# A third landing tile for the feeds of a middle transform stage, and a row norm queued behind the rounding of the row before

## The chip, the core and the metric

One core of a Trainium2 chip runs the whole program. The metric is the device time of one launch in microseconds (us). The engines have separate queues, each run in order: TensorE (PE; its weight loads are shown as PEld), VectorE (DVE), ScalarE (ACT), GpSimd (POOL) and SyncE (SP). A transfer is issued from the queue of SP, ACT or POOL, and all transfers share the core's 16 DMA engines.

## The reference

Four layers of two kinds are interleaved on x of 2048 rows and 576 columns, each with a layer norm ahead of it and a residual around it. Layer A is a two-dimensional Fourier transform by matrices, of which the real part is kept. Layer B is a short convolution of k, a product with v, a long convolution in the frequency domain, and a gate q, which is the normed x here; k, v and the kernels are inputs.

```
def A(x):   a = x @ hid_re.T;  b = x @ hid_im.T
            return seq_re @ a - seq_im @ b
def B(q):   kv = short_conv(k, shift_k) * v
            y  = irfft(rfft(kv, 2S) * rfft(ssm_k, 2S))[:S] + kv * ssm_D
            return q * y
x = x + A(norm(x));  x = x + B(norm(x));  x = x + A(norm(x));  x = x + B(norm(x))
```

The long convolution's result y depends on no x, so it is computed once and used in both B layers. All inputs are float32, and matrix products are made to nearly that precision.

## The kernel before

*Precision.* Every matrix operand is split into a rounded high part (ACT, a copy that rounds) and a low part (DVE, the difference); a product is then three matmuls: high x high, high x low, low x high. `split` (line 94, its operations at lines 95 and 96) does it for the c matrices of the sequence transform and for results; `to_x` (lines 188 to 194) does it for a row of x: rounding at line 190 on ACT, the difference at lines 192 and 193 on DVE.

*The main stream.* `layer` (line 306) runs the first A layer: 4 blocks of 512 outputs by 2 (real, imaginary) by 16 steps. A step loads one c tile (`load_c`, line 209, from the SP queue), splits it, and multiplies it with one row tile of x: 14 matmuls of 512 columns. In the first 16 steps the row tiles themselves are made: `get_x0` (line 680) loads a tile, takes its statistics, ends its norm (`next(ln, 0)`, line 689, which issues the scaling on ACT at line 186 for the first eight tiles, at line 665 for the others) and splits it with `to_x`. It works up to three tiles ahead of the step (XLEAD). The last A layer, from about 760 us on, uses seven products in place of eight.

*The side stream.* Between the matmuls of the main stream a generator, `branch` (line 353), computes the long convolution as a transform in three stages, a piece at each `yield`. A pacing loop (lines 761 to 780) advances it by the step of the main stream.
- The first stage (names f1r, f1f; f1_split, f1_products) takes the rows of ssm_k and of the short convolution, which runs on DVE at lines 398 and 403, multiplies them by constants f1c and stores the results to a DRAM tensor t, half by half (lines 454 and 455, issued on ACT).
- The middle stage (tile `mid`) has 64 pieces of work. Each reads one 128x576 piece of t, a "feed": `load_feed` issues its load on SP behind the latest c load (`load_after`, line 161) into a landing tile, `split_feed` makes its two halves (ACT at line 512 or 514, DVE at line 518), `mid_kernel` multiplies one column half and copies it about on ACT, `mid_signal` multiplies the other and combines both on DVE (lines 531 to 534), and `mid_round` and `mid_inverse` transform back and store to vd.
- The last stage ("i2") reads vd in 32 feeds by the same ring of landing tiles; `i2_products` multiplies a feed with constants i2c that `load_fc` brings from the POOL queue (`load_fr`, line 165) into a ring "fc" of two tiles. The first of these feeds comes behind 38 of the middle stage's, and from there every third is one.

*Rings and places.* Tiles lie at hand-chosen places in a few large buffers; `lay` (line 128) appends such places to a named ring, and a ring gives its tiles out in turn. In the middle stage "land" has two tiles, in `flts`, and "fc" has two, at the end of the buffer `mid` (lines 491 to 495). A feed's load waits for the split of the feed that had its tile.

*What sets the order.* The engines' orders are made by a scheduler from the order of the code and the dependences; `behind(...)` (line 99) and `load_after` add the rule that an instruction stands behind a given one. Lists hold such instructions: `rounded` the roundings of line 190, `stored` the last copies of line 454, `halved`, `evac` and `added` others.

Of the kernel before, what the change touches and what calls it, by code (L numbers as in the profile page):

```python
# [10 lines left out]
F32 = mybir.dt.float32  # L11
# [4 lines left out]
P = 128  # L16
S = 2048
D = 576
# [28 lines left out]
I2_FIRST = 37  # L47
# [21 lines left out]
def fnet_h3_kernel(ctx: ExitStack, tc: tile.TileContext, x, c_mat, w_re, w_im, k_pad, v, shift_k,  # L69
# [28 lines left out]
    @contextmanager  # L98
    def behind(*instructions):
        with ExitStack() as stack:  # L100
            for i in instructions:
                stack.enter_context(tc.issue_after(i))
            yield
# [11 lines left out]
    def region_b(dt, name):  # L115
        return sb.tile([P, 6 * WIDE], dt, tag="rb", name=name)
# [9 lines left out]
    ring = {}  # L126

    def lay(t, at, *sizes):

        for name, words, n in sizes:  # L130
            ring.setdefault(name, Ring()).tiles.extend(t[:, at + i * words:at + (i + 1) * words] for i in range(n))
            at += n * words
        assert at <= t.shape[1], (at, t.shape, sizes)
        return at

    def fresh(*names):
        for name in names:
            ring[name] = Ring()
# [20 lines left out]
    anchor, made, rounded, pows, biased, halved, added, evac, parted, stored = [], [], [], [], [], [], [], [], [], []  # L159

    def load_after(dst, src):
        with tc.issue_after(anchor[-1]):
            return nc.sync.dma_start(dst, src).ins

    def load_fr(dst, src):
        with tc.issue_after(pows[-1]):
            nc.gpsimd.dma_start(dst, src)
# [20 lines left out]
    def to_x(y, j):  # L188
        t = xs[:, j, :]
        rounded.append(nc.scalar.activation(t[:, :D], y, AF.Copy).ins)  # L190
        h = t.bitcast(F32)
        nc.vector.tensor_tensor(t[:, D:D + REM], y[:, NC * P:], h[:, NC * P:D], OP.subtract)
        made.append(nc.vector.tensor_tensor(t[:, D + REM:], y[:, :NC * P], h[:, :NC * P], OP.subtract).ins)
        return t
# [155 lines left out]
    def quads(v):  # L350
        return v.rearrange("p (a q) -> p a q", a=4)

    def branch():
# [3 lines left out]
        at = lay(flts, SC_AT + CRAW * NT, ("so", D, 4), ("land", D, 3))  # L357
# [126 lines left out]
        m1 = region_b(FR, "mid")  # L484
        kk_at = SC_AT + CRAW * NT + 4 * D
        at = lay(m1, 0, ("df", 2 * D, 3), ("mc", 4 * P, 1))
# [4 lines left out]
        ring["craw"].tiles.extend(held)  # L491
        spare = at
        at = lay(m1, at, ("yf", D, 2))
        lay(m1, at, ("fc", 4 * P, 2))
        at = lay(flts, SC_AT + CRAW * NT, ("res", D, 2))
        lay(flts, at, ("land", D, 2), ("kk", D, 2), ("vo", HD, 3), ("p2", HD, 1))
        mc = quads(ring["mc"]())
# [22 lines left out]
        def mid_kernel(df):  # L520
            pk, kk = mid_half(df, HD), two(ring["kk"]())
            act(kk[:, 0, :], pk[:, :HD], AF.Copy)
            act(kk[lo, 1, :], kk[hi, 0, :], AF.Copy)
            act(kk[hi, 1, :], kk[hi, 0, :], AF.Copy, scale=-1.0)
            act(kk[hi, 0, :], kk[lo, 0, :], AF.Copy)
            return kk

        def mid_signal(df, kk):
            px = mid_half(df, 0)
            p1, p2 = kk[:, 0, :], ring["p2"]()  # L530
            nc.vector.tensor_tensor(p1, px[:, :HD], p1, OP.mult)
            nc.vector.tensor_tensor(p2[lo], px[hi, :HD], kk[hi, 1, :], OP.mult)
            nc.vector.tensor_tensor(p2[hi], px[lo, :HD], kk[lo, 1, :], OP.mult)
            nc.vector.tensor_tensor(p1, p1, p2, OP.add)
            return p1

        def mid_round(p1):
            yf = two(ring["yf"]())
            act_split(yf[:, 0, :], yf[:, 1, :], p1)
            return yf  # L540

        def mid_inverse(hf, qg, yf):
            pv = bank()
            mm(pv[:, :HD], mc[:, 2, :], yf[:, 0, :], True, False)
            mm(pv[:, :HD], mc[:, 2, :], yf[:, 1, :], False, False)
            mm(pv[:, :HD], mc[:, 3, :], yf[:, 0, :], False, True)
            vo = ring["vo"]()
            act(vo, pv[:, :HD], AF.Copy)
            nc.scalar.dma_start(v_d[hf][4 * qg:4 * qg + 4].rearrange("q j c d -> (q j c) d"), vo)

        def i2_products(hf, j, fc, vf):
            yo = ring["vo"]()
            ps = bank()
            for c in range(2):
                cs = slice(c * HD, (c + 1) * HD)
                mm(ps[:, :HD], fc[:, c, :], vf[0][:, cs], c == 0, False)
                mm(ps[:, :HD], fc[:, c, :], vf[1][:, cs], False, False)
                mm(ps[:, :HD], fc[:, 2 + c, :], vf[0][:, cs], False, c == 1)
            act(yo, ps[:, :HD], AF.Copy)
            nc.scalar.dma_start(yb_d[j][:, hf * HD:(hf + 1) * HD], yo)  # L560
# [13 lines left out]
        def load_feed(i):  # L574
            if i < len(feeds):
                kind, hf, q = feeds[i]
                landed[i] = ring["land"]()
                load_after(landed[i], v_d[hf][:, q].rearrange("p c d -> p (c d)") if kind else
                           t_d[hf][4 * q:4 * q + 4].rearrange("x h j s d -> (x h j) (s d)"))

        def load_fc(k):
            if k < len(rows):
                fcs[k] = quads(ring["fc"]())
                load_fr(fcs[k], i2c[rows[k]])

        def split_feed(i):
            if i < len(feeds):
                halves[i] = parts("df")
                act_split(*halves[i], landed.pop(i))

        load_feed(0)
        load_feed(1)
        yield 0
        for i in range(2):
            split_feed(i)
            load_feed(i + 2)
            load_fc(i)
        used, ahead, product = 0, 2, None
        for i, (kind, hf, q) in enumerate(feeds):
            df = halves.pop(i)  # L600
            if kind:
                i2_products(hf, q, fcs.pop(used), df)
                load_fc(used + ahead)
                used += 1
            else:
                if len(yfs) == MID_LAG:
                    mid_inverse(*yfs.pop(0))
                    yield 0.4
                kk = mid_kernel(df)
                if product is not None:  # L610
                    yfs.append((*product[:2], mid_round(product[2])))
                yield 1.6
                product = hf, q, mid_signal(df, kk)
            split_feed(i + 2)
            load_feed(i + ahead + 2)
            if i == last_mid:
                yield 0.4
                mid_inverse(*yfs.pop(0))
                yfs.append((*product[:2], mid_round(product[2])))
                while yfs:  # L620
                    yield 0.4
                    mid_inverse(*yfs.pop(0))
                for name, t, at, words in (("fc", m1, spare, 4 * P), ("land", flts, kk_at, D)):
                    old = ring[name]
                    held = [old.tiles[(old.n + m) % 2] for m in range(2)]
                    fresh(name)
                    lay(t, at, (name, words, 2))
                    ring[name].tiles.extend(held)
                for m in range(2):
                    load_fc(used + ahead + m)  # L630
                    load_feed(i + ahead + 3 + m)
                ahead = 4
            yield I2_COST if kind else 1.1

    def sums(src, junk):
# [33 lines left out]
    def load_x(j):  # L669
        if j < J:  # L670
            XL[j] = ring["x"]()
            nc.sync.dma_start(XL[j], x[:, j, :])

    def stats0(j):
        if j < J and j not in LN:
            src = XL.pop(j)
            LN[j] = src, normed_x(src, src, ring["junk"]()) if j >= ASTAT else normed(src, src)
            next(LN[j][1])

    def get_x0(j):  # L680
        if X[j] is None:
            if j > 0:
                load_x(j + 2)
            stats0(j)
            if j > 0:
                with behind(*stored):
                    stats0(j + 1)
            src, ln = LN[j]
            next(ln, 0)
            X[j] = to_x(src, j)  # L690

    def done0(j, xa):
# [41 lines left out]
    pending = []  # L734
    lay(flts, SC_AT, ("craw", NT, CRAW))
    br = branch()
    wl = load_w()
    load_x(0)
    next(br)
    get_x0(0)  # L740
    with tc.issue_after(biased[0]):
        next(br)
# [6 lines left out]
    used = 4  # L749
# [3 lines left out]
    with behind(first_lo):  # L753
        get_x0(1)
# [243 lines left out]
    for n, whole in layer(get_x1, lambda j: xb_d[j], done1, pending, 1):  # L998
# [12 lines left out]
        if n == STATIC:  # L1011
            t7.append(region_a(FR, "t7"))
            at = lay(flts, SC_AT + CRAW * NT, ("csum", WIDE, 3), ("rems", 2 * REM, 2))
# [132 lines left out]
```

## Time and profile before

| what | value |
|---|---|
| runs of the kernel, three | 1206.66, 1211.91, 1214.1 us; median 1211.91 us |
| the profiled execution, its own time | 1212.36 us |
| its span, first to last instruction | 1210.6 us |
| mean granted TensorE clock in it | 0.995 of full |
| busy share: PE, PEld, DVE, ACT, POOL | 97%, 84%, 72%, 57%, 6% |
| moved by DMA | 271.38 MB, mean 224 GB/s |
| the chain that ended last, by engine | PE 73%, DVE 9%, ACT 7%, DMA 6%, issue 4% |

A time in a row of the timeline is that from the span's start. Such a row reads: start, duration, engine (with q: issued by its sequencer, a transfer), line, operation, output<-inputs, shape, count, and in brackets the engine's idle time just before and what ended it. The releaser is inferred, and where several were waited for it is the last one by the clock. A row "L96" or "L163" is the line of a helper, so the tile names tell what it is: "flts<-t" from SP is a feed's load, "flts<-in_c_mat" a load of a c tile, "mid<-in_i2c" from POOL a load of i2c, and "mid<-flts" on ACT (128x576) the split of a feed. Matmuls overlap in PE's pipeline: with work at hand those of 512 columns follow each other every 0.226 us, though one lasts 0.39.

### The profile page before, as it was taken

What the parts mean: (1) busy time and instruction counts of PE and PEld (TensorE: products, weight loads), DVE (VectorE), ACT (ScalarE), POOL (GpSimd) and SP (SyncE); (2) the same over time, 40 slices, a digit from 0 to 9 for tenths busy, and PEclk for the clock granted to TensorE, in tenths of its full rate; (3) what the DMA queues carried; (4) which work ended last, traced back from release to release, by engine and by line L of the source; (5) the groups of instructions that cost most, each with busy time, mean ns of one, the idle gap of its engine ahead of it and who ended that gap; (6) DMA issues with size and microseconds to landing.
All of it is one profiled execution on the core that took longest, in us unless ns stands there. A gap on an engine that the chain in (4) does not pass through costs nothing.

```text
span 1210.6 us, 18119 instructions
## 1 busy us (share of the span) xinstructions
PE 1175.5 (97%) x6192; PEld 1011.4 (84%) x6192; DVE 870.4 (72%) x1531; ACT 684.6 (57%) x1366; POOL 71.2 (6%) x116
## 2 busy tenths in 40 slices
PE   7999999989999999999999999999999999999997
PEld 5877788869888887888888898788888888889997
DVE  7799999668787777777346766775776777774764
ACT  7955666667787687767455667534444445450210
POOL 2100000000000000000111111000000000001111
PEclk9999999999999999999999999999999999999999
DMA  8878797885477477766986777873683587795621
GB/s 289 284 213 244 243 324 238 305 259 153 149 232 267 136 200 251 239 194 217 336 263 224 236 240 238 268 254 92 178 289 99 178 288 266 239 331 154 224 91 40
DMA packets 148702, 271.38 MB, mean 224 GB/s; under 512 B 16129, under 2 KB 45057, under 8 KB 148610
## 3 DMA queue, kind: packets, MB, share of 16 engines
q1 hardware_dynamic: 105266, 215.02, 55.3%
q10 hardware_dynamic: 36432, 42.63, 10.2%
q0 software_dynamic: 6912, 12.59, 4.0%
q8 instruction: 48, 0.79, 0.3%
q14 instruction: 44, 0.36, 0.1%
HBM read 198.81 MB, written 71.37 MB: 223 GB/s over the span
## 4 chain that ended last, share of the span: by engine, by line
PE 73%; DVE 9%; ACT 7%; DMA 6%; issue 4%; SPq 0%; POOL 0%; ACTq 0%; POOLq 0%; DVEq 0%
PE s L78 41%; PE bk L78 29%; PE rm L78 4%; ACT flts L512 3%; DVE f1f L398 2%; DMA flts<-in_c_mat 1%; DMA t<-flts 1%; DVE f1f L403 1%; DMA flts<-t 1%; DVE mats L96 1%; ACT mats L95 1%; ACT mid L512 1%; DVE f1r L442 1%; DVE mid L518 1%; DVE u L96 1%
## 5 line engine op out<-in xcount | busy, mean ns | idle before, releaser
L78 PE MATMUL s<-mats 128*128 128x512 f32 x2088 | 537.7, 394 | 6.5 <-DVE u L96 2.7
L78 PEld LDWEIGHTS s<-mats 128*128 128x128 f32 x2088 | 385.2, 189 | 82.4 <-DVE u L96 3.6
L95 ACT ACTIVATE mats<-flts 128x512 fp32r<-128x512 f32 x206 | 128.3, 628 | 84.9 <-PE bk L78 30.4
L96 DVE TENSOR_TENSOR mats<-flts,mats 128x512 fp32r<-128x512 f32 x206 | 140.6, 689 | 48.3 <-ACT mats L95 47.2
L78 PE MATMUL bk<-mid 128*128 128x288 f32 x768 | 134.8, 304 | 11.0 <-ACT flts L512 4.9
L78 PEld LDWEIGHTS bk<-mid 128*128 128x128 f32 x768 | 113.4, 188 | 34.0 <-ACT flts L512 15.8
L518 DVE TENSOR_TENSOR mid<-flts,mid 128x576 fp32r<-128x576 f32 (+1 forms) x160 | 102.1, 638 | 41.8 <-ACT mid L512 31.7
L78 PE MATMUL bk<-w,u 128*128 128x288 f32 x864 | 120.6, 295 | 1.1 <-ACT flts L512 0.9
L78 PEld LDWEIGHTS bk<-w,u 128*128 128x128 f32 x864 | 117.3, 188 | 4.4 <-ACT flts L512 2.3
L512 ACT ACTIVATE flts<-bk 128x288 f32<-128x288 f32 x160 | 61.2, 403 | 73.3 <-PE bk L78 59.1
L512 ACT ACTIVATE mid<-flts 128x576 fp32r<-128x576 f32 (+1 forms) x159 | 87.1, 582 | 17.0 <-DMA flts<-t 10.8
L78 PE MATMUL rm<-mats 128*128 128x512 f32 x304 | 95.8, 392 | 0.5 <-DVE flts L269 0.5
L512 ACT ACTIVATE flts<-flts 64x288 f32<-64x288 f32 x192 | 85.0, 443 | 6.2 <-ACT flts L512 0.2
L454 ACT ACTIVATE flts<-bk 128x288 f32<-128x288 f32 x128 | 46.7, 408 | 38.1 <-PE bk L78 33.2
L78 PE MATMUL bk<-mats 128*128 128x288 f32 (+1 forms) x376 | 67.8, 317 | 0.0
L78 PEld LDWEIGHTS rm<-mats 128*128 128x128 f32 x304 | 57.2, 189 | 12.6 <-PE s L78 0.9
L78 PE MATMUL s<-t,mats 128*128 128x512 f32 x264 | 64.9, 389 | 0.0
L283 DVE TENSOR_TENSOR flts<-flts,bk 128x288 f32<-128x288 f32 x48 | 21.8, 453 | 55.9 <-PE bk L78 55.1
L78 PE MATMUL bk<-mats,t 128*128 128x288 f32 (+1 forms) x368 | 59.3, 303 | 0.0
L179 POOL TENSOR_TENSOR flts<-flts 128x1 f32<-128x1 f32 x35 | 28.5, 813 | 514.7 <-DVE flts L178 514.7
L78 PEld LDWEIGHTS bk<-mats 128*128 128x128 f32 x376 | 55.6, 188 | 3.4
L78 PEld LDWEIGHTS s<-t,mats 128*128 128x128 f32 x264 | 49.5, 188 | 10.4 <-DVE t L96 0.2
(145 smaller groups left out, 1516.0 us busy)
## 6 DMA issues: line engine op xcount, KB each, us to landing
flts<-in_c_mat SPq DMA_DIRECT2D x148, 256.0 KB, 3.8
ph<-in_c_mat SPq DMA_DIRECT2D x54, 512.0 KB, 4.0
t<-flts ACTq DMA_DIRECT2D x64, 288.0 KB, 4.5
flts<-t SPq DMA_DIRECT2D x64, 288.0 KB, 3.1
flts<-in_c_mat SPq DMA_DIRECT2D x30, 512.0 KB, 5.3
vd<-flts ACTq DMA_DIRECT2D x64, 144.0 KB, 2.5
flts<-vd SPq DMA_DIRECT2D x32, 288.0 KB, 5.0
mid<-in_i2c POOLq DMA_DIRECT2D x32, 256.0 KB, 5.8
```

Source lines behind the costliest of these rows:

```text
L78: nc.tensor.matmul(ps, lhsT, rhs, start=first, stop=last, skip_group_check=more)
L95: a = nc.scalar.activation(h, src, AF.Copy).ins
L96: return a, nc.vector.tensor_tensor(l, src, h.bitcast(F32), OP.subtract).ins
L179: pows.append(nc.gpsimd.tensor_tensor(rs, ve, mhalf, OP.pow).ins)
L283: added[:] = [nc.vector.tensor_tensor(r[:, cs], r[:, cs], ps[:, :HD], OP.add).ins]
L398: nc.vector.tensor_tensor(out_t[:, n], k, wt[3 - t][:, n], OP.mult)
L403: nc.vector.tensor_tensor(rp, rp, out_t, OP.add)
L442: parted[:] = h + [nc.vector.tensor_tensor(t[to], r[at], t[at].bitcast(F32), OP.subtract).ins for t, at, to in sides]
L454: stored[:] = [nc.scalar.activation(so[:, h, :], ps[:, :HD], AF.Copy).ins]
L512: last_act.append(nc.scalar.activation(*args, **kw).ins)
L518: nc.vector.tensor_tensor(l, src, h.bitcast(F32), OP.subtract)
```

## The change

Two edits. The first lets the middle stage start with three landing tiles. The third tile takes the place at the end of `mid` that the two fc tiles had, which are not laid out until later; the two loads of i2c at the start of the stage go. Three feeds are loaded at the start, and then each feed's load is issued one feed earlier than before: behind the split of feed i+2, feed i+5 in place of i+4. From feed 29 on, as soon as the tile next in turn is the third one (that is at feed 30), the ring goes back to its other two tiles, the fc tiles are laid out, the two i2c loads are issued, one load is left out, and all goes on as before. The second edit puts the end of a row's norm (`next(ln, 0)`) behind the rounding of the row before it.

```
@@ branch @@
-        lay(m1, at, ("fc", 4 * P, 2))
+        fc_at = at
...
-        load_feed(0)
-        load_feed(1)
+        third = m1[:, fc_at:fc_at + D].bitcast(F32)
+        ring["land"].tiles.append(third)
+        for i in range(3):
+            load_feed(i)
         yield 0
         for i in range(2):
             split_feed(i)
-            load_feed(i + 2)
-            load_fc(i)
-        used, ahead, product = 0, 2, None
+            load_feed(i + 3)
+        used, ahead, feed_ahead, product = 0, 2, 3, None
...
             split_feed(i + 2)
-            load_feed(i + ahead + 2)
+            if i >= I2_FIRST - 8 and feed_ahead == 3:
+                tiles = [ring["land"]() for _ in range(3)]
+                if tiles[0] is third:
+                    ring["land"], feed_ahead = Ring(tiles[1:]), 2
+                    lay(m1, fc_at, ("fc", 4 * P, 2))
+                    load_fc(0)
+                    load_fc(1)
+            if feed_ahead == 2:
+                feed_ahead = 2.5
+            else:
+                load_feed(i + int(feed_ahead) + 2)
...
-                ahead = 4
+                ahead = feed_ahead = 4
@@ get_x0 @@
-            next(ln, 0)
+            with behind(*rounded[-1:]):
+                next(ln, 0)
             X[j] = to_x(src, j)
```

## The prediction

> **What bounds the kernel now.** I read the page first, for the busy shares; then busy time by stretch, for the places where TensorE stands still; then the timeline and the waits of those places; then the instruction orders of the two programs, which show what the edits move.
>
> ```profile
> PE 1175.5 (97%) x6192; PEld 1011.4 (84%) x6192; DVE 870.4 (72%) x1531; ACT 684.6 (57%) x1366; POOL 71.2 (6%) x116
> ...
> L512 ACT ACTIVATE mid<-flts 128x576 fp32r<-128x576 f32 (+1 forms) x159 | 87.1, 582 | 17.0 <-DMA flts<-t 10.8
> ```
>
> TensorE (PE) is busy for 1175.5 of 1210.6 us. No edit touches a matmul, so all that can be won is idle time of PE, 35.1 us, and time in which its clock is low. The second row is the work that the landing tiles feed: ACT's splits in the middle stage idled 10.8 us for transfers. Busy time by stretch (stretch, length, then busy us of PE, PEld, DVE, ACT and POOL, the granted clock, the DMA share, GB/s) tells where that is:
>
> ```profile
> 0.00:50.00 50.00, 42.03 (x175) 33.74 (x176) 33.96 (x105) 41.78 (x81) 10.81 (x21) 1.00 0.87 307
> 50.00:70.00 20.00, 17.63 (x81) 14.24 (x79) 17.68 (x30) 14.88 (x30) 2.13 (x3) 1.00 0.67 197
> 70.00:140.00 70.00, 67.03 (x306) 53.92 (x307) 68.86 (x82) 40.68 (x82) 3.18 (x6) 0.98 0.76 227
> 140.00:248.00 108.00, 107.44 (x533) 91.05 (x532) 90.00 (x109) 73.48 (x153) 4.24 (x8) 1.00 0.89 288
> 248.00:275.00 27.00, 22.94 (x101) 17.77 (x100) 17.59 (x32) 17.63 (x34) 0.00 (x0) 0.94 0.81 247
> 275.00:403.00 128.00, 125.59 (x745) 110.09 (x745) 100.65 (x203) 97.85 (x222) 0.00 (x0) 1.00 0.62 196
> 403.00:600.00 197.00, 190.67 (x1103) 166.32 (x1102) 139.18 (x268) 140.84 (x308) 12.19 (x23) 1.00 0.73 225
> 600.00:1210.60 610.60, 602.14 (x3159) 524.25 (x3157) 402.46 (x709) 257.44 (x460) 38.64 (x55) 1.00 0.65 211
> ```
>
> Length less PE busy: 8.0 us idle up to 50, 2.4 up to 70, 3.0 up to 140, 0.6 up to 248, 4.1 in the 27 us in which the middle stage opens, 2.4 in its first part, 6.3 in its second, 8.5 in the second half of the program. The two orders differ only up to about 130 us and from 254 to 403 us; behind that every engine runs the same list. So the change has some 20 us of idle within its reach, much of it the start (first loads), which it does not touch.
>
> **The change part by part.** *The norm behind the rounding (line 689).* Rows of the first layer are normed (line 186, later 665) and rounded (line 190) on ACT. Now the norm of a row stands behind the rounding of the row before. At the start ACT runs two norms ahead of the rounding that PE waits for:
>
> ```profile
> 13.04 1.81 ACT L186 ACTIVATE early<-early,flts 128x576 f32<-128x576 f32 x2 [2.35 <-DVE flts L185]
> 14.76 0.67 ACT L190 ACTIVATE mats<-early 128x576 fp32r<-128x576 f32 x1
> 15.48 0.73 PE L78 MATMUL s<-mats 128*128 128x512 f32 x2 [0.30 <-ACT mats L190]
> ```
>
> One of the two (half of 1.81) moves back, so the rounding comes 0.9 us sooner; PE only waited 0.30 for it: -0.3 us. In exchange the rounding of the row after comes behind two splits (line 95); PE works for over 3 us on the row in between, which covers that. The larger place is row 14 of 16:
>
> ```profile
> 59.09 0.78 ACT L640 ACTIVATE early<-early,flts 128x576 f32<-128x576 f32 x1 [1.58 <-DVE flts L639]
> 60.07 0.39 PE L78 MATMUL rm<-mats 128*128 128x512 f32 x1
> 61.05 0.16 DVE L664 TENSOR_TENSOR flts<-flts 128x1 f32<-128x1 f32 x1 [0.66 <-POOL flts L642]
> 61.30 0.87 ACT L665 ACTIVATE early<-early,flts 128x576 f32<-128x576 f32 x1 [0.59 <-DVE flts L664]
> 62.07 0.67 ACT L190 ACTIVATE mats<-early 128x576 fp32r<-128x576 f32 x1
> 62.77 0.23 DVE L192 TENSOR_TENSOR mats<-early,mats 128x64 fp32r<-128x64 f32 x1 [1.57 <-ACT mats L190]
> 62.79 3.02 PE L78 MATMUL s<-mats 128*128 128x512 f32 x12 [1.81 <-ACT mats L190]
> 63.22 0.61 ACT L95 ACTIVATE mats<-flts 128x512 fp32r<-128x512 f32 x1
> ```
>
> PE idles 1.81 us for the rounding at 62.07, which stands behind the norm of row 15 at 61.30, which waited 0.59 for its bias. In the new order a split of the c matrix (0.61, line 95) stands there instead, and it can't start before PE ends the step whose buffer it takes (60.07+0.39=60.46). The rounding then starts at about 60.5+0.6=61.1 and not 62.07: -0.95 us. Can it be kept? VectorE is the bound from 50 to 140 (68.86 of 70 us): what PE wins it keeps only as far as DVE comes forward, and DVE has 0.66+1.57 us of idle here to give up, which is enough. Together -1.2 us. Ends: -2.7 (0.30, all of 1.81, and the 0.56 below, where DVE's new order puts line 96 of the first evacuation one operation earlier) and +0.9 (one norm's 0.87 falling ahead of some other rounding that PE waits for).
>
> ```profile
> 70.00 0.50 PE L78 MATMUL s<-mats 128*128 128x512 f32 x1 [0.56 <-DVE u L96]
> ```
>
> *The opening of the middle stage.* Three feeds are loaded at once and the two i2c loads that stood at the start are gone until feed 30. SP and ACT in the timeline, with the idle time before each operation:
>
> ```profile
> 243.59 1.07 POOL L167 DMA_DIRECT2D mid<-in_i2c  x2
> 249.96 0.33 SPq L163 DMA_DIRECT2D flts<-t  x1
> 253.50 0.86 SPq L163 DMA_DIRECT2D flts<-in_c_mat  x2
> 253.75 0.68 ACT L514 ACTIVATE mid<-flts 128x576 fp32r<-128x576 f32 x1 [6.29 <-DMA flts<-t]
> 257.19 0.58 SPq L163 DMA_DIRECT2D flts<-t  x1
> 257.86 0.68 ACT L512 ACTIVATE mid<-flts 128x576 fp32r<-128x576 f32 x1 [1.25 <-DMA flts<-t]
> 260.77 0.63 ACT L95 ACTIVATE mats<-flts 128x512 fp32r<-128x512 f32 x1 [1.47 <-DMA flts<-in_c_mat]
> 263.35 0.90 ACT L512 ACTIVATE flts<-flts 64x288 f32<-64x288 f32 x2
> 265.23 0.45 DVE L533 TENSOR_TENSOR flts<-bk,flts 64x288 f32<-64x288 f32 x1
> 265.83 0.37 PE L78 MATMUL bk<-mid 128*128 128x288 f32 x1 [1.59 <-ACT mats L95]
> ```
>
> Feed 0 is issued at 249.96, when the last store that it reads has landed, and PE's first mid matmul follows it. DMA issues of the stretch 243 to 250, then of 254 to 258 (count, KB each, median us to landing):
>
> ```profile
> DMA packets 1237, 2.01 MB, mean 287 GB/s; under 512 B 103, under 2 KB 514, under 8 KB 1237
> ...
> t<-flts ACTq DMA_DIRECT2D x2, 288.0 KB, 6.7
> ```
> ```profile
> t<-flts ACTq DMA_DIRECT2D x1, 288.0 KB, 7.2
> ...
> flts<-in_c_mat SPq DMA_DIRECT2D x1, 256.0 KB, 6.7
> ```
>
> Without the two i2c loads, 0.52 MB less is in flight ahead of that store; at 287 GB/s this is up to 1.8 us, and nothing if the store isn't held by them. I take 1.2, since the stretch is near full (0.9 of the engines). Against it stands what the third load is moved past: on SP it takes the place of the second c load (253.50, x2), which goes behind two w loads to the place of 257.19, 3.2 us later. Landing 6.7 us after issue, it comes at 257.2-1.2+6.7=262.7. Its split (260.77) is put behind five more ACT operations, ahead of the last of the two at 263.35. ACT would get there at about 263.35+0.45-0.63=263.2 (one of the two done, the split itself not yet run), with the stage 1.2 us forward at 262.0, and waits 0.7 in place of the 1.47 before. Behind this wait stand that last operation, the split of feed 2, and through line 533 the bank that PE's 265.83 really waits for (line 533 ends at 265.68; the releaser named is only the last by clock). So -1.2+0.7, and -0.3 as an estimate for the evacuations of PE's banks that no longer stand behind the 1.47: -0.8 us. Ends: -5.7 (the 4.1 idle, and the 1.6 that a clock of 0.94 costs in 27 us) and +2.9 (worked out below).
>
> The clock drops here once:
>
> ```profile
> 266.00:270.40 4.40, 4.07 (x13) 3.30 (x13) 4.12 (x9) 4.27 (x10) 0.00 (x0) 0.61 0.62 200
> ```
>
> That is 4.4 x 0.39 = 1.7 us lost behind an idle of 1.59. I leave the drop in, since PE still idles a like time before it. The Trainium skill ("TensorE: Matmul & The Clock Gate", What's actually happening) has the clock halved after an idle window of about 3.4 us; no single idle of this trace ahead of the drop is that long, so the trace does not agree. By that rule the drop would not hang on waits of this length: a longer one would not deepen it and a shorter one not remove it, which moves two of the rivals below.
>
> *Three tiles, steady.* From feed 3 to feed 32 each load is issued where the load of one feed earlier stood, so nothing is added to SP, and one feed time is won in lead (4.1 us between the splits at 253.75 and 257.86). One wait of this part is for a feed, the other such waits come behind 403 us (second fence, ACT's waits of 403 to 620: total, times, longest), where the third tile is given back:
>
> ```profile
> 366.11 0.69 ACT L512 ACTIVATE mid<-flts 128x576 fp32r<-128x576 f32 x1 [1.34 <-DMA flts<-t]
> ...
> 367.44 0.80 PE L78 MATMUL bk<-mid 128*128 128x288 f32 x4 [0.90 <-ACT flts L512]
> ```
> ```profile
> ACT mid L512 <- DMA flts<-t: 8.2, 6, 2.8
> ```
>
> 1.34 is less than the 4.1 of lead, so the wait goes and PE's 0.90 with it: -0.9 us (ends 0 and -1.3). The 8.2 us of later waits stay.
>
> *Giving the tile back.* At feed 30 one load is left out and two i2c loads go to POOL. The first i2 product stands 8 feeds later, some 33 us against landings of up to 7.2 us in the rows above: 0 us. If a feed were late here it would cost one more 0.9.
>
> **Sum.** -1.2 -0.8 -0.9 = -2.9 us on the profiled 1212.36 us gives 1209.5. The median of the runs, 1211.91, is 0.45 lower: 1209.0.
>
> **Rivals.** *The c load that gives way to the third feed holds up the opening (slower).* If nothing lands sooner, it is issued at 257.2 and lands 6.7 to 7.2 us later, at 263.9 to 264.4. ACT stands before its split from 263.2 on (worked out above), and a landing behind that decides. The last operation of the pair then ends at 264.4+0.63+0.45=265.5 and not at 264.25, PE idles 1.2 us more, and a second clock drop of 1.7 may follow: +2.9. With the other terms 1212.36-1.2+2.9-0.9=1213.2, or 1212.7 by the median. Against it: 0.52 MB less in flight ahead of all these loads. By the rule of the Trainium skill on the clock the 1.7 would not come, and this rival would end at 1211.0.
>
> *The third tile is idle.* The opening hangs on the store and the w loads, and one late feed is replaced by another late thing: only -1.2 stays, 1211.2, by the median 1210.7. For it: 8.2 of the 10.8 us that ACT waits for feeds outside the first one lie behind 403.
>
> *The opening closes almost whole (faster).* If feed 2 and the kernel chain come early enough for the idle before 265.83 to fall under what drops the clock, and the drop in 70 to 140 (clock 0.98 there, 1.4 us) goes as well, -4.9 (of the 5.7 above; 0.8 stays) and -1.4 take the place of -0.8: 1212.36-1.2-6.3-0.9=1204.0, by the median 1203.5. Against it: all of feed 0's 6.29 can't go, as its store comes first. By the same rule of the Trainium skill neither drop would go (1.7 and 1.4), and this rival would end at 1206.6.
>
> **How the numbers follow.** Forecast 0.50, third tile idle 0.19, opening whole 0.18, c load late 0.13. The forecast's own range is 1206 to 1212. The range takes in the faster and the slower case with the bounds of the early part: 1202 to 1215.5. A measurement of this kernel can tell about 1% (12 us) from no change, as three runs of one program lie 7 us apart. No case as priced reaches that: below 1199.8 lies only the tail of the faster case with the early bound (1204.0-1.5, less what 403 to 600 might give), 0.10; above 1224 only further clock drops on top of the slower case, 0.06; the rest 0.84.
>
> **What would show it.** Row 14: PE's idle of 1.81 near 62 falls below 1.0, with a line 95 between norm and rounding. Opening: feed 0's load issued by 249 in the span's time; the split behind 260.77 waits for c under 0.6; PE's idle in its 27 us falls from 4.1 to 3.3 or less. No ACT wait for a feed between 270 and 400; those behind 403 stay near 8 us. I am wrong if PE's idle before its sixth mid matmul grows over 2 us, if feeds are late at the place where the tile is given back, or if the stretches behind 403 change by over 2 us, where no order changes.

## The result, and the profile after

The changed kernel takes 1216.04 us (median of 15 runs, 1211.91 to 1217.56). The kernel before, run beside it, takes 1210.32 us (15 runs, 1206.66 to 1214.10). The ratio is 1.0040, with an interval of 1.0029 to 1.0051: slower by half a per cent, 5.7 us by the medians (4.9 by the means), where 1209.0 was forecast.

The profiled execution after took 1216.06 us, its median. That of before took 1212.36 us, 2.0 us above its median here, so the two traces show 3.7 of the 5.7 us. Busy time by stretch of the changed kernel, with the columns of the prediction's table:

```profile
0.00:50.00 50.00, 41.12 (x169) 31.66 (x170) 32.98 (x101) 40.68 (x77) 10.29 (x20) 1.00 0.86 296
50.00:70.00 20.00, 16.46 (x71) 13.42 (x70) 15.45 (x31) 12.84 (x27) 3.21 (x4) 0.93 0.74 225
70.00:140.00 70.00, 66.08 (x309) 54.02 (x308) 68.06 (x80) 42.32 (x83) 3.17 (x6) 0.99 0.73 219
140.00:248.00 108.00, 106.99 (x528) 90.28 (x529) 90.94 (x110) 71.35 (x150) 3.07 (x6) 1.00 0.85 281
248.00:275.00 27.00, 23.19 (x93) 18.15 (x92) 17.56 (x29) 18.47 (x36) 0.10 (x1) 0.88 0.89 268
275.00:403.00 128.00, 127.38 (x761) 112.49 (x760) 102.09 (x206) 98.15 (x222) 1.05 (x2) 1.00 0.61 195
403.00:600.00 197.00, 189.16 (x1086) 165.10 (x1086) 138.54 (x267) 141.07 (x310) 11.08 (x21) 0.99 0.72 221
600.00:1214.30 614.30, 606.48 (x3184) 528.59 (x3182) 404.37 (x712) 259.95 (x466) 39.29 (x57) 1.00 0.64 213
sum 1214.30, PE 1176.86 PEld 1013.71 DVE 869.99 ACT 684.82 POOL 71.27; mean PE 147.11 PEld 126.71 DVE 108.75 ACT 85.60 POOL 8.91
```

PE is busy 1.4 us longer than before (the same matmuls, more of them at half clock) and idles 37.4 us instead of 35.1. By stretch, idle grew from 8.0 to 8.9 up to 50 us and from 2.4 to 3.5 in the next 20, where the clock fell to 0.93. It shrank from 2.4 to 0.6 between 275 and 403.

A stretch of fixed time holds other work once a kernel is late, so I use a second measure: **PE's lag**, the start of PE's k-th matmul after, less that of the k-th before. Both programs have the same 6192 matmuls, though near 60 us and near 260 us their order differs a little.

| matmul | 1 | 21 | 101 | 201 | 231 | 251 | 601 | 1001 | 1201 | 1801 | 2351 | 2951 | last |
|---|---|---|---|---|---|---|---|---|---|---|---|---|---|
| its time before, us | 7.2 | 15.5 | 33.9 | 55.9 | 63.8 | 68.4 | 149 | 229 | 277 | 380 | 475 | 586 | 1202 |
| lag after, us | 0.1 | -0.7 | 1.45 | 1.4 | 3.2 | 4.8 | 2.9 | 4.5 | 4.0 | 2.6 | 6.1 | 4.8 | 3.8 |

So the loss is made in the first 70 us, by the norm edit: 1.4 us up to the 101st matmul, 1.7 at row 14, 1.6 behind it. The middle stage gains a little, the feeds behind 403 us lose again. Here is row 14 (timeline of the changed kernel; its lines 649 to 676 were 638 to 665):

```profile
59.07 7.33 SPq L163 DMA_DIRECT2D flts<-in_c_mat  x4
...
60.41 0.78 ACT L651 ACTIVATE early<-early,flts 128x576 f32<-128x576 f32 x1 [1.04 <-DVE flts L650]
...
61.19 0.86 ACT L676 ACTIVATE early<-early,flts 128x576 f32<-128x576 f32 x1
...
64.70 0.63 ACT L95 ACTIVATE mats<-flts 128x512 fp32r<-128x512 f32 x1 [2.65 <-DMA flts<-in_c_mat]
...
65.23 0.67 ACT L190 ACTIVATE mats<-early 128x576 fp32r<-128x576 f32 x1
...
65.81 0.86 ACT L676 ACTIVATE early<-early,flts 128x576 f32<-128x576 f32 x1
65.95 4.28 PE L78 MATMUL s<-mats 128*128 128x512 f32 x12 [3.54 <-ACT mats L190]
```

The order is the predicted one: norm of row 14 (61.19), split of a c tile, rounding of row 14, norm of row 15. But the split waits 2.65 us for its c tile to land, and ACT's queue holds the rounding behind it. PE idles 3.54 us instead of 1.81. The twelve matmuls then take 4.28 us instead of 3.02, because the clock drops to half.

### The profile page after: what moved, and what is told of

The parts are those of the page before. It is cut to its first block, busy times and chain, and to the rows that moved or that the text cites. A ratio compares the mean times of both kernels' runs of the same rounds, so it can differ in the third digit from the quotient of the medians.

```text
span 1214.3 us, 18129 instructions
## 1 busy us (share of the span) xinstructions
PE 1176.9 (97%) x6192; PEld 1013.7 (83%) x6192; DVE 870.0 (72%) x1531; ACT 684.8 (56%) x1366; POOL 71.3 (6%) x116
## 4 chain that ended last, share of the span: by engine, by line
PE 75%; DVE 10%; DMA 7%; ACT 5%; issue 3%; SPq 0%; POOL 0%; ACTq 0%; POOLq 0%; DVEq 0%
PE s L78 42%; PE bk L78 28%; PE rm L78 4%; DMA flts<-in_c_mat 3%; ACT flts L512 2%; DVE mats L96 2%; DMA flts<-t 2%; DVE f1r L442 1%; DVE f1f L398 1%; DVE f1f L403 1%; DVE mid L518 1%; ACT mid L512 1%; DMA flts<-vd 1%; ACT mats L95 1%; DVE u L96 1%
## 5 line engine op out<-in xcount | busy, mean ns | idle before, releaser
L518 DVE TENSOR_TENSOR mid<-flts,mid 128x576 fp32r<-128x576 f32 (+1 forms) x149 | 93.7, 629 | 39.4 <-ACT mid L512 32.1
L512 ACT ACTIVATE mid<-flts 128x576 fp32r<-128x576 f32 (+1 forms) x148 | 80.5, 575 | 16.2 <-DMA flts<-t 9.0
```

Source lines behind the costliest of these rows:

```text
L512: last_act.append(nc.scalar.activation(*args, **kw).ins)
L518: nc.vector.tensor_tensor(l, src, h.bitcast(F32), OP.subtract)
```

## The experiments

The runs were made in three batches on three chips, each with the kernel before beside it: e1, e2, e4, e6 (before's median 1210.78 us), then e3, e7, e8, e9 (1211.41), then e5, e11, e12, e13 (1209.23). Kernels of different batches can be compared only through their distance to before. The ratio is not that of the medians (for e6 it stands for 2.7 us, the medians for 1.3); where the two differ, go by the ratio and its interval. "Wait" is PE's idle before row 14's matmuls (two numbers: before its first and its fifth matmul); "half" counts windows of half clock between 64 and 72 us; the lags are at matmul 201 and 271.

| kernel | wait, us | half | lag 201 | lag 271 | median less before's, us | ratio (interval) |
|---|---|---|---|---|---|---|
| before (profiled) | 1.81 | 0 | - | - | - | - |
| changed kernel | 3.54 | 1 | 1.4 | 4.2 | +5.7 | 1.0040 (1.0029 to 1.0051) |
| e1 norm edit alone | 3.49 | 2 | 1.8 | 5.3 | +3.7 | 1.0041 (1.0024 to 1.0059) |
| e2 tile edit alone | 1.84 | 1 | 0.4 | 1.4 | -1.65 | 0.9987 (0.9968 to 1.0007) |
| e3 norm, rows 0 to 7 | 3.51 | 2 | 1.2 | 4.8 | +4.6 | 1.0040 (1.0026 to 1.0054) |
| e4 norm, rows 8 to 15 | 2.43 | 1 | 0.4 | 2.0 | +0.8 | 1.0002 (0.9985 to 1.0020) |
| e7 norm, rows 0 to 2 | 3.80 | 1 | 0.7 | 3.7 | +2.6 | 1.0018 (1.0005 to 1.0032) |
| e6 both, split behind | 0.40+0.59 | 0 | 2.0 | 2.7 | +1.3 | 1.0022 (1.0005 to 1.0040) |
| e8 as e4, split behind | 0.55 | 0 | 0.9 | -0.7 | -0.4 | 0.9994 (0.9981 to 1.0007) |
| e9 as e8, and tile | 0.51 | 0 | 0.5 | -1.2 | -1.6 | 0.9984 (0.9971 to 0.9996) |
| e11 norm, c tile early | 0.77+0.85 | 0 | 1.75 | 1.7 | +4.2 | 1.0037 (1.0023 to 1.0052) |
| e13 only c tile early | 1.81 | 0 | 0.1 | 0.1 | +2.85 | 1.0031 (1.0018 to 1.0044) |
| e12 both, c tile early | 0.76+0.85 | 0 | 1.55 | 1.6 | +2.6 | 1.0018 (1.0005 to 1.0030) |
| e5 late i2c, two tiles | 1.83 | 1 | 0.6 | 1.5 | +1.45 | 1.0012 (0.9999 to 1.0024) |

Lags under 0.5 us are the scatter of the first loads: the first matmul comes between 7.1 and 7.7 us in these traces.

**Each edit alone.** e1 has only the second edit of the diff, e2 only the first.

> Only the second edit: the norm behind the rounding of the row before, two landing tiles and early i2c loads as before. Theory N (the loss is the new order of the first 16 rows: the split of c tile 16 stands ahead of row 14's rounding on ScalarE and waits for its transfer): slower than the kernel before by 3.5 to 6 us, with TensorE's idle before row 14 near 3.5 us as in the changed kernel. Rival T (the third tile and its giving back lose the time, in the late feeds behind 403 us): within 1.5 us of the kernel before.

> Only the first edit: third landing tile, i2c loads late. Theory N: faster than the kernel before by 1 to 2.5 us (0.4 at the opening, 1.2 at the wait near 366 us, both as the changed kernel showed them). Rival T: slower by 2 to 4 us, with the 2.8 us lost between 460 and 485 us in the changed kernel there again.

The norm edit alone is as slow as the changed kernel by its ratio (1.0041 against 1.0040), with its 3.49 us at row 14. The tile edit alone is 1.65 us faster by the medians, which its interval doesn't tell from nothing. The tile is not the cause; rival T falls. Added up, the two medians give +2.05 us where both edits together measured +5.7. The ratios multiply to 1.0028 against 1.0040, within their intervals, so it stays open whether the two edits cost more together than apart.

**Which rows.** e4, then e3 and e7, keep the norm edit for some rows only:

```
-            with behind(*rounded[-1:]):
+            with behind(*rounded[-1:] if j >= ASTAT else ()):     # e4; ASTAT is 8
+            with behind(*rounded[-1:] if j < ASTAT else ()):      # e3
+            with behind(*rounded[-1:] if j <= 2 else ()):         # e7
```

> The second edit for rows 8 to 15 alone, nothing of the first edit. ScalarE's order differs from the kernel before only from row 12 on: the split of c tile 16 moves ahead of row 14's rounding, the norm of row 15 behind it; the first rows are as before. Theory N: slower by 1.5 to 4 us, the idle before row 14 over 2.3 us. Rival S (the loss is in the first rows, where the order of roundings and splits changed by 1.4 us up to 40 us): within 1 us of the kernel before, the idle before row 14 at 1.8 us or less.

> The norm edit for rows 0 to 7 only, neither tile nor anything of rows 8 to 15. Its ACT order still has the split of c tile 16 ahead of row 14's rounding, so the exchange at row 14 comes from the order of the first rows as well. Theory N (the loss is made of a start that is 1.4 us late by 35 us, and of a split that is late by what the start made its transfer late): PE is 1.3 to 1.9 us later than before at matmul 200, the wait at row 14 is 3 to 3.6 us against 1.81, and the time is that of the whole norm edit, 1213 to 1216. Rival M (rows 8 to 15 themselves carry the loss, by their own order): the time is that of before, 1209.5 to 1212, as the start's lag is absorbed where DVE bounds, at 137 us.

> The norm edit for rows 0 to 2 only: the one place for which the prediction had a gain of 0.3 us at the start. Its ACT order has the exchange at row 14 too. Theory N with the loss of the start in the rows behind 2: row 1 is rounded 0.8 us sooner, PE is 0.3 to 0.8 us ahead of before at matmul 20 and keeps it to matmul 100, and the wait at row 14 is 2.4 us as with rows 8 to 15 alone; 1209.5 to 1212. Rival P (moving row 2 alone makes the planner pack the next rows anew, and the loss of the start is there already): ahead at matmul 20, 1 us or more behind at matmul 100, a wait of 3 us or more at row 14, and 1212.5 to 1215.5.

e4 has the exchange at row 14 on time, and costs little. Its ACT shows why (timeline):

```profile
60.31 0.86 ACT L665 ACTIVATE early<-early,flts 128x576 f32<-128x576 f32 x1
62.59 0.63 ACT L95 ACTIVATE mats<-flts 128x512 fp32r<-128x512 f32 x1 [1.42 <-DMA flts<-in_c_mat]
...
63.12 0.67 ACT L190 ACTIVATE mats<-early 128x576 fp32r<-128x576 f32 x1
```

The split waits 1.42 us and not 2.65, since the c tile is there sooner. Its wait at row 14 (2.43 us) is N's, its time (+0.8 us) rival S's. In its trace the lag of 2.0 at matmul 271 is down to 0.4 by 149 us, because PE's wait of 1.92 us before 137.55 is not followed by half clock, where before's of 1.93 is (137.09 to 140.50); the last section tells why. Theory N in its first form put the loss here, and rival S in the first rows; each is half of it, and from e3 on N stands for both together. e3, with nothing changed for rows 8 to 15, has the full loss, as N then expected: its scheduler makes the same exchange at row 14 as a consequence of the first rows' order, and the tile is late as well. e7 is nearer to its rival P: moving rows up to 2 alone leaves 0.7 us of lag at matmul 201 and 3.80 us of wait at row 14. So the first rows matter twice: they make PE 0.7 to 1.4 us late, and they make the c tile land later. The second shows on SP, in the timelines of before and after:

```profile
55.76 0.33 SPq L423 DMA_DIRECT2D flts<-in_v  x1
57.75 0.33 SPq L163 DMA_DIRECT2D flts<-in_c_mat  x1
```
```profile
55.02 0.33 SPq L423 DMA_DIRECT2D flts<-in_v  x1
57.73 0.33 SPq L377 DMA_DIRECT2D f1f<-in_k_pad  x1
59.07 0.33 SPq L163 DMA_DIRECT2D flts<-in_c_mat  x1
```

The load waits for its buffer, free at 57.7 before and 59.05 after (the ends of line 96 in the two timelines). And a load of k_pad, issued at 53.39 before, now stands 1.3 us ahead of it. DMA issues of before (57.5 to 59) and after (58.5 to 60), the last column being us to landing:

```profile
flts<-in_c_mat SPq DMA_DIRECT2D x1, 256.0 KB, 4.3
```
```profile
flts<-in_c_mat SPq DMA_DIRECT2D x1, 256.0 KB, 5.5
```

It lands at 62.06 before and at 64.6 after, 2.5 us later. 1.3 of it is the buffer; 1.2 is a slower transfer, which I put down to the 576 KB of k_pad ahead of it. The other traces agree: this place's c load takes 5.5 to 6.0 us in all seven kernels in which k_pad is issued 1.3 us ahead of it, 4.2 to 4.5 in six of the seven others and 2.8 in e5. No run moved k_pad alone.

**The split behind the rounding.** e6 has both edits, e8 is e4, e9 is e8 with the tile edit; in all three the split of this one tile is put behind row 14's rounding:

```
     def load_c(step):
...
-        with behind(*stored):
+        with behind(*stored, *(rounded[14:15] if step == (0, 0, 0) or step == (1, 0, 0) else ())):
             halved[:] = split(t[0], t[1], raw)
```

> Both edits, with one rule more: the split of c tile 16 stands behind the rounding of row 14. All engines' orders are those of the changed kernel but for this exchange on ScalarE and its shadow on VectorE. Theory N: the idle before row 14 falls from 3.5 to about 1 us and the clock drop behind it goes, 3 to 4.5 us faster than the changed kernel, so within 1.5 us of the kernel before. Rival S or T: no more than 1 us faster than the changed kernel.

> The norm edit for rows 8 to 15 only, and the split of c tile 16 behind row 14's rounding, so that the ACT order is normalise 14, round 14, normalise 15, split, round 15: the order that the prediction had in mind for its 0.95 us. Theory N: PE's wait at row 14 is about 1.0 us instead of 1.81 before and 2.43 with the split ahead of the rounding; PE stands 0.8 us better than before at matmul 230, too short a wait for a clock drop, and 1208.5 to 1210.5 at the end if what is won there stays. Rival A (the next bound takes it back: the split that now stands behind is late for its own step): PE's next wait grows by the same 0.8 us, no lead by matmul 300, 1210.5 to 1212.

> The same and the third landing tile with the late i2c loads. Theory N (the parts add up): the tile's gain of 1.5 us in the medians, on top of the other: 1207 to 1209.5, the lowest of all kernels here. Rival A (parts ahead of the opening of the middle stage are lost in it, the tile alone decides): 1209 to 1211, like the tile alone (1209.13).

In e6 PE waits 0.40 and 0.59 us at row 14 and no half clock follows, as N expected. By the medians it lies 4.4 us nearer to before than the changed kernel does, by the ratios 2.2, and the two intervals overlap; so N is shown by the wait rather than by the time. e8's timeline, ACT and PE:

```profile
60.78 0.85 ACT L665 ACTIVATE early<-early,flts 128x576 f32<-128x576 f32 x1
...
61.67 0.68 ACT L190 ACTIVATE mats<-early 128x576 fp32r<-128x576 f32 x1
62.26 0.86 ACT L665 ACTIVATE early<-early,flts 128x576 f32<-128x576 f32 x1
...
62.40 3.04 PE L78 MATMUL s<-mats 128*128 128x512 f32 x12 [0.55 <-ACT mats L190]
63.07 0.63 ACT L95 ACTIVATE mats<-flts 128x512 fp32r<-128x512 f32 x1
```

The rounding follows the norm at once, PE's wait falls from 1.81 to 0.55, and the lag from 0.9 to -0.4 between matmuls 201 and 231. The split, at 63.07, waits for nothing. This is the gain that the prediction wanted, though not by its order, which had a split between norm and rounding. At matmul 301 the lag is still -0.6. Rival A's loss comes later, where VectorE bounds (before, then e8):

```profile
135.57 1.64 PE L78 MATMUL s<-mats 128*128 128x512 f32 x6 [1.93 <-DVE u L96]
```
```profile
136.04 1.20 PE L78 MATMUL s<-mats 128*128 128x512 f32 x4 [2.55 <-DVE u L96]
```

PE waits 0.6 us longer there than before (and 1.11 near 114 us in place of 0.63 near 109), and at matmul 601, near 149 us, the lag is +0.5, so of the 1.25 us won at row 14 only 0.4 are left. e9 waits as long there, but its wait is not followed by the half clock that follows in before and in e8, and it keeps its lead. The times of e8 and e9, 1210.99 and 1209.84, lie within A's ranges and not N's, but these ranges were set from the first chip, where before took 0.6 us less; with that taken off, e8 lies in N's and e9 in both. At the end the gain of row 14 can't be seen: e8's interval holds no change. e9 is below before with its whole interval, though by 1.6 us only. Its one difference to e6 is rows 0 to 7, and it lies 2.9 us lower against before by the medians (4.6 by the ratios, on two chips): that is about what the edit of those rows costs where row 14 is mended.

**The tile there in time.** e11 is e1, e12 the changed kernel, e13 the kernel before, each with c tile 16 in a place of its own, so that its load waits for no buffer:

```
     def load_c(step):
         g, tb, k = step
-        raw = ring["craw"]()
+        raw = early[:, 10 * D:10 * D + NT] if len(anchor) == 16 else ring["craw"]()
```

> The whole norm edit, with c tile 16 alone landing in a tile of its own (words of the region of the first rows that nothing uses at that time), so that its load waits for no buffer and is issued one place sooner on SP, ahead of the loads of v and of k_pad. The ACT order is that of the norm edit: normalise 14, split, round 14. Theory N (the split waits for its transfer, not the order itself, makes the loss at row 14): the split waits for no DMA, PE's wait at row 14 falls from 3.49 us to 1.0 to 1.4 us, no half clock follows, PE is 1 to 1.5 us later than before at matmul 250 instead of 5.9, and the time is 1210 to 1212.5. Rival O (the order costs, whatever the transfer does: one split more ahead of the rounding, other engines late with it): a wait of 2.4 us or more, 1213 to 1215.

> Both edits, with c tile 16 in a tile of its own. Theory N: the wait at row 14 is 1.0 to 1.4 us, and 1209 to 1212 in place of 1216. Rival O: 1213.5 to 1216.

> The kernel before with nothing but c tile 16 in a tile of its own: the control of the two above. There the split stands behind both rows' rounding and waited for nothing. Theory N: no change at row 14 (1.8 us), the time within 1.5 us of before. Rival B (the tile helps by itself, as the later c loads come a buffer sooner): 2 us or more below before, and the two runs above owe it that.

This is the direct test, as the ACT order with the split ahead of the rounding stays. e11's timeline:

```profile
61.50 0.86 ACT L665 ACTIVATE early<-early,flts 128x576 f32<-128x576 f32 x1
62.26 0.61 ACT L95 ACTIVATE mats<-early 128x512 fp32r<-128x512 f32 x1
62.78 0.67 ACT L190 ACTIVATE mats<-early 128x576 fp32r<-128x576 f32 x1
63.50 1.20 PE L78 MATMUL s<-mats 128*128 128x512 f32 x4 [0.77 <-ACT mats L190]
...
65.54 2.14 PE L78 MATMUL s<-mats 128*128 128x512 f32 x8 [0.85 <-DVE mats L193]
```

The split waits for no transfer, no half clock follows, and the lag is 1.7 us at matmul 271 instead of 5.3, all of it the start's. So at row 14 theory N holds, and rival O falls. The times say less. That of e12 (1211.83) is N's; that of e11 (1213.39, 4.2 us above before) is in O's range. The control tells why they can't be read alone: e13, with no norm edit, loses 2.85 us to the extra place itself, which neither theory had. Against the control the norm edit costs 1.3 us by the medians, against 3.7 without it, and with each interval some 1.5 to 2 us to either side this difference is not clear of noise.

The clock of e13's runs tells where its loss is. Their mean granted clock is 0.9935, that of before's 31 runs beside it 0.9958; one less the clock, times the span, is the time lost, 7.9 against 5.0 us. This is 2.8 of the 3.1 us by which the means differ. So e13 loses by more half clock, and by little else. What its extra place shifts to bring this about stays open.

**Which half of the tile edit.** e5 moves the i2c loads and keeps two tiles:

```
-        lay(m1, at, ("fc", 4 * P, 2))
+        fc_at = at
...
-            load_fc(i)
...
+            if i == I2_FIRST - 7:
+                lay(m1, fc_at, ("fc", 4 * P, 2))
+                load_fc(0)
+                load_fc(1)
```

> Neither norm edit nor third tile: two landing tiles as before, and only the i2c loads moved from the opening to feed 30, as in the changed kernel. It tells which half of the tile edit gives the 1.65 us of the medians (1209.13 against 1210.78) at the opening of the middle stage and at 366 us. If the freed transfers give it: 1208.5 to 1210.5, the opening about 2 us shorter, the wait at 366 us as in before. If the third tile gives it: 1210 to 1212, the opening and the wait at 366 us as in before.

e5 is 1.45 us above its before, e2 1.65 below its own: the late i2c loads alone bring nothing that shows. At 366 us the lag falls by 0.5 us with e5 and by 1.4 with e2, and by 1.4 in all five kernels that have the third tile, against 0.4 to 1.2 in the eight others. At the opening (matmul 1001 to 1201) it falls by 0.5 us with e5 and 2.2 with e2, but there the kernels without either part of the tile edit differ just as much among themselves, from 0.9 lost (e1) to 2.8 gained (e3), so the opening tells nothing here. Two more pairs on one chip agree with e2's size: e9 is 1.15 us below e8 by the medians, e12 1.6 below e11. The changed kernel against e1, on two chips, doesn't (2.0 above by the medians, level by the ratios). So what gain there is, some 1 to 1.6 us, comes with the third tile as far as these runs show, and each such difference alone lies near the noise.

## Why the prediction was wrong, step by step

**Norm edit, row 14: -0.95 predicted, +1.7 measured, and a half clock of 1.6 behind it. This is the step that failed.** It said that "a split of the c matrix (0.61, line 95) stands there instead, and it can't start before PE ends the step whose buffer it takes (60.07+0.39=60.46)". That priced the buffer which the split writes, and not the landing of the tile that it reads. In before the landing, at 62.06, was hidden: the split ran at 63.22, behind the rounding, and waited for nothing. A split moved 2 us up can't start before 62.06, and the rounding behind it not before 62.6, later than the 62.07 it had: even with nothing else late, the exchange loses. e4 is that case (2.43 us of wait against 1.81). e8, without the split in between, gives the gain that was forecast and more. The prediction's next step, that the gain can be kept because DVE has idle to give up, did not hold either: of e8's 1.25 us 0.4 are left at 149 us. (Its "68.86 of 70 us" is the row of 70 to 140; in 50 to 70 DVE is busy for 17.68 of 20.)

**Norm edit, start: -0.3 predicted, +1.4 measured.** The first part came, larger than forecast by luck: PE's lag is -0.7 at matmul 21. Of this 0.6 stands at matmul 18 already, since the clock came up at 12.79 us in this trace and at 14.21 in that of before (matmuls follow each other every 0.43 us ahead of it, 0.23 behind); without that, the earlier rounding would have been worth the 0.30 that PE had waited for it. The next sentence, "PE works for over 3 us on the row in between, which covers that", priced ACT alone. PE and ACT of the changed kernel:

```profile
14.74 0.74 PE L78 MATMUL s<-mats 128*128 128x512 f32 x2 [0.17 <-ACT mats L190]
...
16.59 2.12 PE L78 MATMUL s<-mats 128*128 128x512 f32 x8 [0.37 <-DVE flts L178]
17.55 0.70 ACT L190 ACTIVATE mats<-early 128x576 fp32r<-128x576 f32 x1
...
19.70 1.89 PE L78 MATMUL s<-mats 128*128 128x512 f32 x7 [0.32 <-DVE flts L178]
...
24.16 2.14 PE L78 MATMUL s<-mats 128*128 128x512 f32 x8 [0.33 <-DVE flts L650]
```

The rounding of the row after is at 17.55, 1.35 us later than before (16.20) and still covered. What isn't covered is DVE: the low halves of rows and c tiles now come behind the statistics of further rows (lines 176 to 178 and 650), and PE stops for them three times, 1.0 us in all, where before stopped once for 0.24 (16.95). In e7, with the edit up to row 2 only, a lag of -0.9 us at matmul 21 turns into one of 0.7 by matmul 101: one moved norm reorders the rows behind it. The slow end that I gave the whole norm edit, +0.9, was too small for either place.

**Opening of the middle stage: -0.8 predicted, -0.45 measured** (lag from 4.5 to 4.0, in a place where single traces differ by more). Feed 0 came sooner:

```profile
253.34 0.33 SPq L163 DMA_DIRECT2D flts<-t  x1
...
256.29 0.69 ACT L514 ACTIVATE mid<-flts 128x576 fp32r<-128x576 f32 x1 [3.49 <-DMA flts<-t]
...
268.96 2.27 PE L78 MATMUL bk<-mid 128*128 128x288 f32 x6 [2.15 <-DVE flts L533]
```

With the lag of 4.5 taken off, feed 0 is issued 1.1 us sooner and split 2.0 sooner than before. PE's idle before 268.96 is 2.15 where it was 1.59, and half the clock is lost behind it for two windows instead of one: 1.7 us given back. The 1.2 us that the prediction gave the two i2c loads don't show by themselves: e5, where they alone are gone, issues feed 0 at 249.91 and splits it at 253.68 with a lag of -0.1, like before. What brings feed 0 forward here stays open.

**Late feed at 366 us: -0.9 predicted, -1.4 measured.** ACT has no wait for a feed between 270 and 403 us, as forecast, in any kernel with the third tile. Before's trace loses most there, so part of the 1.4 is that trace: the other kernels without the tile gain 0.4 to 1.2 against it.

**Giving the tile back: 0 predicted, up to 3.5 lost behind it, of which 1.4 had come back by 586 us.** No order differs there. ACT's waits from 403 to 620 (total, times, longest), and the worst place:

```profile
ACT mid L512 <- DMA flts<-t: 9.0, 6, 3.2
ACT mid L512 <- DMA flts<-vd: 3.6, 3, 2.4
```
```profile
476.48 0.67 PE L78 MATMUL bk<-mid 128*128 128x288 f32 x3 [1.95 <-ACT flts L512]
```

The waits for t grew from 8.2 to 9.0 us, those for vd from 2.9 to 3.6. PE's idle at 476.48 was 0.70 before; a half clock from 477.0 to 480.4 adds 1.7. In e2 the same stretch lost 1.3 us without a half clock, and in the eight kernels without the third tile 0.5 to 1.9. Since single traces differ there by such amounts, I don't count it to the change.

**The sum.** The two tile terms, -1.7 together, stand beside -1.65 measured (e2); that they meet so closely is luck, as e2's interval reaches from 3.9 us faster to 0.8 slower. The norm term, -1.2, stands beside +3.7 (e1; 5.0 by its ratio). The error is that one term. No rival named it. The one on the slow side had the right mechanism, a transfer that an in-order queue waits for, but at the opening of the middle stage.

## What to carry to other kernels

Before an instruction is moved up in an in-order queue, list everything it reads with the time at which each thing is there, the landing of its transfer first: an operation that waited for nothing may have been hidden by the very work that it is moved past. An order rule given to a scheduler acts beyond the place that it names; compare the whole order that comes out, the loads too, and price every place where it differs. A run with the rule on a few rows only (e7), or with the moved instruction held back (e8), tells which part of such a change loses.

## What the runs showed of the hardware

The clock drops by the window, a fixed stretch of 3.41 us. Busy time in four stretches of the changed kernel, e1, the changed kernel's opening, and e2 (the last three columns are clock, DMA share and GB/s):

```profile
67.40:70.80 3.40, 3.40 (x9) 2.64 (x9) 3.35 (x4) 0.10 (x1) 0.00 (x0) 0.50 0.68 228
```
```profile
64.65:71.50 6.85, 5.27 (x12) 4.13 (x13) 4.88 (x7) 2.65 (x4) 0.00 (x0) 0.50 0.77 245
```
```profile
268.70:275.60 6.90, 6.52 (x17) 5.26 (x18) 6.33 (x13) 6.21 (x14) 0.00 (x0) 0.51 0.79 243
```
```profile
64.50:67.90 3.40, 3.40 (x10) 2.66 (x9) 3.40 (x4) 0.00 (x0) 0.00 (x0) 0.50 0.71 226
```

Half clock lasted one window, two, or once three (e12, from 257.1 us) wherever a trace has it ahead of the program's end, so it costs 1.7 us per window of work. Waits of 1.83 (e5) and 1.84 us (e2) were followed by one, waits of 1.81 (before, e13) were not, and neither was one of 2.55 us in the changed kernel at 140. What tells them apart is where they lie in the windows. In each trace the half clocks begin on one grid of 3.413 us. Counted back from where they begin (137.09 in before, 64.72 in e5), the windows at row 14 are these, before first:

```profile
58.58:62.00 3.42, 2.40 (x13) 1.84 (x11) 1.96 (x7) 2.33 (x4) 1.07 (x2) 1.00 0.81 224
62.00:65.41 3.41, 2.62 (x11) 2.16 (x12) 2.64 (x5) 1.83 (x4) 0.00 (x0) 1.00 0.97 321
```
```profile
61.31:64.72 3.41, 1.58 (x8) 1.12 (x7) 1.54 (x5) 2.54 (x4) 0.80 (x2) 1.00 0.73 226
64.72:68.13 3.41, 3.41 (x10) 2.62 (x9) 3.33 (x4) 0.00 (x0) 0.00 (x0) 0.50 0.81 270
```

A border cuts before's wait into 1.02 us of idle and 0.79. The wait of e5 lies in one window, 1.83 idle of its 3.41, and the next window runs at half clock. In the changed kernel the 3.54 us are 1.57 ahead of the border at 63.99 and 1.96 behind it, and half clock comes with the next window, at 67.40, 1.4 us after the wait's end. In e1 1.97 us lie ahead of the border at 64.71, and half clock begins there, while PE still waits. The 2.55 us near 140 are cut into 1.63 and 0.92. The 14 traces have 4820 windows at full clock up to 1195 us. All 23 with 1.83 us of idle or more were followed by half clock; of the others, with 1.80 or less, two were (1.45 in e8, 1.53 in e12). Behind a window already at half clock this doesn't decide: in the changed kernel 0.3 us of idle (from 268.8) was followed by a second one.

So the same wait costs 1.7 us or nothing by where a border falls, and that differs from trace to trace. Before's runs lie 7 to 13 us apart in a batch, with clocks of 0.992 to 0.999; how much of this scatter is the clock was not worked out. The Trainium skill ("TensorE: Matmul & The Clock Gate", What's actually happening) describes a free-running activity window of about 3.4 us and one idle window ahead of the lower clock. The length and the grid agree with these traces. The prediction took from it that the drop would not hang on waits as short as these, and that does not hold here: a little over half a window of idle was enough.
